# Seven-product 2x2 blocks for three more products of a fused attention and SwiGLU kernel, and silu in one ScalarE operation

## The chip, the cores and the metric

One NeuronCore of a Trainium2 chip. The metric is the device time of one execution in microseconds; less is better. Engines are named as in the profile: PE is TensorE, PEld its weight loads, DVE VectorE, ACT ScalarE, POOL GpSimd, SP the queue that issues most DMAs.

## The reference

```python
# q, k, v: 4 batches, 8 heads, 768 positions, 64 wide; heads 0, 2, 6 see all earlier keys,
# the others see the first 4 keys and the last 64
scores = scale * np.matmul(q, k.transpose(0, 1, 3, 2))
scores = np.where(mask[None, :, :, :], scores, -1000000000.0)
a = softmax(scores)
attn_out = np.matmul(a, v)
x = attn_out.transpose(0, 2, 1, 3).reshape(B * S, H * D)     # 3072 tokens x 512
g = x @ w_gate                                               # 512 x 1536
silu = g * (1.0 / (1.0 + np.exp(-g)))
val = x @ w_val                                              # 512 x 1536
out = (silu * val) @ w_out                                   # 1536 x 512
```

## The kernel before, in words

Attention runs in 24 tiles of 128 queries. For a tile, PE multiplies keys with queries into PSUM (`scores`, line 567), ACT takes the exponential (579), DVE or POOL multiply a mask in (587), PE multiplies with the values (597), DVE divides by the sum (604, 605), and the result is turned by PE (621) or by a DMA (615) into `xt`, the columns of x for the second part. Four tiles make a group of 512 tokens; there are six groups.

For a group, `gate` (759) computes 12 blocks of 128 rows of g and 12 of val, each with four matmuls of 128x128 weights and 512 columns into one bank of PSUM. The silu is computed as g (1 + tanh(g/2)) / 2: ACT takes the tanh (765), DVE multiplies (1 + tanh) by g (769, `stt1`), and a second DVE operation (775, `stt2`) multiplies by 0.5 and val into `h_sb`. The output product of a group is already done in 2x2 blocks with seven products instead of eight (`seventh`, line 860, matmuls of 256 columns): `hsum` (831) makes four sums of blocks of h on DVE or POOL, `wsum` (412) made the sums of blocks of w_out once, and `gathered` (886, 890, 898) adds the seven results into the four blocks of the output, which are stored by DMA.

Every piece of work is a `Task` with the engines it may run on, the tasks it waits for and the buffers it takes from rings. The order in which tasks are issued, the engine of each and the buffer it gets are three tables of digits at the head of the file (`ORDER`, `WAYS`, `SLOTS`), written by a planner beforehand. Each engine works through its own instructions in that order, and semaphores hold it where an input or a buffer isn't ready. The eight banks of PSUM are shared by the rings gv, o and big: a `gate` block holds its bank until the DVE operation that reads it last is done. Tasks of one group are mixed with attention of later ones and output products of earlier ones; the attention ends at about 161 us.

Of the kernel before, what the change touches and what calls it, by code (L numbers as in the profile page):

```python
# [7 lines left out]
FP = mybir.dt.float32  # L8
# [8 lines left out]
    "06000307090A0401081U0D1V1cy11W1X0C1d1f1e0B2021021g280g1i2229231h2B2A1j0m1r2C0h1Y1p1s2D1a0F1Z2N1q"  # L17
    "2X1b1k2E0G2O1l2W1t1m2F1u2L1x1v1w2f2M1n2g2c1y1oxk2h0n27242d25262e2l2i2m2G1z0E0y2H2I2P0z2Q2j8e2R2t"
    "8o0k8f112o2x8p8g302p108q2U312J0i132V8h2K8r2y050H8t8s8y8i8u2k983C8w8v8m323D8j2n2z3I0q8k9D8x991493"
    "3J8l9A3L8z8n94380l91903K96950o2Z9E929B3M979G2Y9F0I3N9C3U339H1C3R3V2a2q2r0j342b9h2s3S162u3O3W9c9i"  # L20
    "0r3T3X9j359d363b9I3P0J3E372v9J3Q3f3i1D2w9N9e0K1F3A9O9f3B3g2S3H9k0p179P3G0v9m9g393F9l9Q9n3h0s3Y3j"
    "9K3Z0u199r3u3a3c3n9R0x3l9s401G3k3m0w9L3o0L3d9M9S3v419o9u2T9t0M9T3p429U433w3q9v441A9p3r450R4C493e"
    "1B469q4A9X4H3y3s4B9Y9a479Z9V3t4D9b3x4Q4N4K9W4OAu9z480O4LAQ9y1H18AnA00tB2Av124RAz1EAw0P4EB0A1BE4Z"
    "B1Ap4V4Y4gB34FBH4GBF0NAxAq1Q1K4hBGAV5CArAkAWBIB41IAl0QAX1J15AY4eAy1S4IB7AZAm0SALAR3z4JAoB51MAs4d"
    "AS9wAt4f1RAM5DANB91TB69x5KBCB8BA4b5fBBAa0WBD5I4o4i4l4P4pA2A45l4m1LA34M5FAT0U1N5E4S5L1PAUAf4jA5A8"
    "1OAg4v5JAbAh4a4k4TAcAE5g4UA95n4y514q4c4zAAA60V4r0a6KACAB5o5GA7AF4WAdAD524n4sAGAiAeAK540TAj505T55"
    "4t5mAO4u5U5MAP565W4x5753AHBM4wBLBJBN5NAI5c5VAJ58595XBO4XBR5A5H5O5BBK5v5p5sBP5wBX5q5Y0YBQ600Z5r5Z"
    "5t5a0XBV5b6I5u6366BWCb6E6HBS645iCe5h6N67BY5PBTCC6O5QBbCD5R7O5d6PCM6wCc6v5xCd0cBZ68CECN71BcCF6JBa"
# [26 lines left out]
SLOTS = (
    "001423105578362145403027124360570705626241030877537806901020040702261213013460614010320001264002"
    "430101642120400017524426503000204102434011162426123000254004600122630164212045422322214400101000"
    "130234502420041024003014523602204224610042412422404222212503602112240050221240143404020044225200"
    "005411611104105112030140001212061231013100700167007612020117123450061751067110011241201016300460"
    "216005211560201025311267261606003611020071110012121267117601100231114700730027201774112050100016"  # L60
    "610661265014600771040126102070067023342264511137001010641241015202110066116102500050001512722100"
    "4111232013411120253127611561005111201141005015610026745406"
# [57 lines left out]
def kernel(  # L120
# [253 lines left out]
    T_w = {}  # L374
# [392 lines left out]
    def stt1(g, j, c):  # L767
        sl[g, j, c] = buf("sil", [128, 512], FP, "sil")[:, 0:c[1] - c[0]]
        nc.vector.scalar_tensor_tensor(  # L769
            out=sl[g, j, c], in0=sg.pop((g, j, c)), scalar=1.0, op0=ALU.add,  # L770
            in1=gs.pop((g, j, c)), op1=ALU.mult)

    def stt2(g, j, c):
        hs[g, j] = h_sb[:, g % 2, j]
        nc.vector.scalar_tensor_tensor(  # L775
            out=hs[g, j][:, c[0]:c[1]], in0=sl.pop((g, j, c)), scalar=0.5, op0=ALU.mult,
            in1=vs.pop((g, j, c)), op1=ALU.mult)
# [251 lines left out]

    for g in range(NG):  # L1030
        w = SIZES[g] * 128
        xs = [T_xe[t] for t in range(FIRST[g], FIRST[g + 1])]
        T_h = {}
        for j in range(NJ):
            parts = [(0, 256), (256, 512)] if g == 0 and j < HALVES else [(0, w)]
            for c in parts:
                a = P.add(f"gate{g}.{j}.{c[0]}", ["PE"],
                          (lambda g=g, j=j, c=c: gate(g, j, c, wg_sb, gs)),
                          deps=xs[c[0] // 128:c[1] // 128] + [T_w["g", j // 2][j % 2]],
                          takes=["gv"])  # L1040
                th = P.add(f"tanh{g}.{j}.{c[0]}", ["ACT"],
                           (lambda g=g, j=j, c=c: tanh(g, j, c)), deps=[a], takes=["sig"])
                s1 = P.add(f"stt1 {g}.{j}.{c[0]}", ["DVE"],
# [9 lines left out]
                T_h.setdefault(j, []).append(s2)  # L1053
                P.uses(a, "gv", s1)
                P.uses(v_, "gv", s2)
                P.uses(th, "sig", s1)
                P.uses(s1, "sil", s2)
                P.uses(T_first_x[g], "xt", a, v_)
        if g < SEVENS:
# [68 lines left out]
```

## Time and profile before

| what | before |
|---|---|
| median of 3 runs | 239.07 us (239.04 to 239.14) |
| profiled execution | 239.03 us |
| its span, first to last instruction | 237.2 us |
| PE / PEld busy | 230.5 / 146.0 us |
| DVE / ACT / POOL busy | 194.5 / 141.2 / 110.6 us |
| granted PE clock | 1.00 |
| DMA | 40.73 MB, mean 172 GB/s |

The profile is of one execution. An engine is busy while at least one of its instructions is in it; matmuls overlap, so their mean duration is longer than their spacing. "Idle before" is the engine's idle time just ahead of an instruction, with what ended it. The time outside the span (1.83 us here) belongs to the execution but to no instruction.

### The profile page before, as it was taken

To read this page: it belongs to the slowest core of one execution; us is meant where nothing else is said; L and a number is where in the kernel's file an instruction comes from. 1 tells how busy PE (TensorE), PEld (TensorE's weight loads), DVE (VectorE), ACT (ScalarE), POOL (GpSimd) and SP (SyncE) were. 2 spreads that over 40 slices of the span, in tenths; PEclk is the share of its full clock that TensorE was granted. 3 is DMA by queue.
4 is the path that set the end of the run, shared out by engine and by line. 5 is a ranking of instruction groups with operands and counts; after the bars stand their busy time and mean duration, and the time that the engine had idled before them with its cause. 6 is when DMAs were issued, how large, how long until landed. Compare 5 with 4: busy or idle time off the path is not lost.

```text
span 237.2 us, 5639 instructions
## 1 busy us (share of the span) xinstructions
PE 230.5 (97%) x2211; PEld 146.0 (62%) x2211; DVE 194.5 (82%) x362; ACT 141.2 (59%) x217; POOL 110.6 (47%) x132
## 2 busy tenths in 40 slices
PE   7899999999999999999999999999999999999994
PEld 2577865655457778655464557766555565557883
DVE  2689999998999699698968989786969867788873
ACT  3699999889599879839575485384242232231010
POOL 7386577937484940998600550884000000525500
PEclk9999999999999999999999999999999999999999
DMA  6999999999999999999798124011620000220044
GB/s 173 351 343 366 326 346 356 358 350 296 271 238 165 236 291 182 289 164 188 196 171 207 34 48 87 4 22 20 203 44 0 3 0 0 87 92 1 20 183 155
DMA packets 67194, 40.73 MB, mean 172 GB/s; under 512 B 25184, under 2 KB 61024, under 8 KB 67168
## 3 DMA queue, kind: packets, MB, share of 16 engines
q1 hardware_dynamic: 65248, 37.50, 63.4%
q10 hardware_dynamic: 1920, 2.88, 3.3%
q8 instruction: 17, 0.28, 0.5%
q14 instruction: 9, 0.07, 0.1%
HBM read 28.31 MB, written 6.29 MB: 146 GB/s over the span
## 4 chain that ended last, share of the span: by engine, by line
PE 92%; DVE 3%; DMA 2%; ACT 1%; issue 0%; DVEq 0%
PE banks L759 51%; PE banks L860 23%; PE banks L567 8%; PE banks L597 6%; PE banks L473 2%; DMA raw<-in_q_dram 2%; PE banks L621 1%; DVE wt_sb L412 1%; DVE sil L769 1%; ACT hq L206 0%; PE banks L321 0%; DVE kT L208 0%; DVE hq L212 0%; DVE qT L208 0%; DVE xb L605 0%; DVE h_sb L775 0%
## 5 line engine op out<-in xcount | busy, mean ns | idle before, releaser
L765 ACT ACTIVATE sig<-banks 128x512 f32<-128x512 f32 (+1 forms) x76 | 42.7, 574 | 54.6 <-PE banks L759 47.5
L759 PE MATMUL banks<-xt,wg_sb 128*128 128x512 f16 (+1 forms) x304 | 71.4, 368 | 0.5 <-DVE sil L769 0.5
L759 PE MATMUL banks<-xt,wv_sb 128*128 128x512 f16 (+1 forms) x304 | 70.9, 368 | 0.0
L579 ACT ACTIVATE e<-banks 128x1024 f16<-128x1024 f32 (+2 forms) x68 | 59.5, 910 | 15.0 <-PE banks L567 6.3
L769 DVE SCALAR_TENSOR_TENSOR sil<-sig,banks 128x512 f32<-128x512 f32 (+1 forms) x76 | 48.8, 655 | 14.3 <-ACT sig L765 13.6
L775 DVE SCALAR_TENSOR_TENSOR h_sb<-sil,banks 128x512 f16<-128x512 f32 (+1 forms) x76 | 48.9, 655 | 2.8 <-PE banks L759 1.8
L860 PEld LDWEIGHTS <-h_sb 128*128 128x128 f16 x420 | 40.4, 98 | 8.5
L759 PEld LDWEIGHTS <-wv_sb 128*128 128x128 f16 x304 | 28.6, 98 | 26.9
L759 PEld LDWEIGHTS <-wg_sb 128*128 128x128 f16 x304 | 28.1, 98 | 27.2 <-issue 0.8
L587 POOL TENSOR_TENSOR e<-e,m 128x640 f16<-128x640 f16 (+1 forms) x17 | 28.0, 1655 | 19.8 <-ACT e L579 19.4
L831 POOL TENSOR_TENSOR h_sb<-h_sb 128x768 f16<-128x768 f16 x13 | 21.2, 1640 | 22.5 <-DVE hs_sb L831 16.7
L898 DVE TENSOR_TENSOR out_sb<-banks,out_sb 128x512 f32<-128x512 f32 x37 | 25.1, 688 | 7.4 <-PE banks L860 7.0
L860 PE MATMUL banks<-wt_sb,h_sb 128*128 128x256 f16 x216 | 26.2, 273 | 0.0
L831 POOL TENSOR_TENSOR hs_sb<-h_sb 128x768 f16<-128x768 f16 x3 | 4.9, 1639 | 45.1 <-PE banks L860 41.2
L860 PE MATMUL banks<-wo_sb,h_sb 128*128 128x256 f16 x204 | 25.1, 273 | 0.0
L597 PEld LDWEIGHTS <-e 128*128 128x128 f16 x472 | 18.0, 97 | 5.8 <-DVE e L587 0.2
L567 PEld LDWEIGHTS <-kT 64*128 64x128 f16 x472 | 14.4, 94 | 9.3 <-issue 8.7
L567 PE MATMUL banks<-qT,kT 64*128 64x128 f16 x472 | 19.7, 218 | 0.2 <-ACT qT L206 0.2
L597 PE MATMUL banks<-vt,e 128*128 128x65 f16 x472 | 19.7, 193 | 0.1
L206 ACT CAST hq<-raw 128x1024 f16<-128x1024 f32 (+1 forms) x16 | 14.7, 936 | 5.2 <-DMA raw<-in_q_dram 3.2
L605 DVE TENSOR_TENSOR xb<-banks,rc 128x512 f16<-128x512 f32 x24 | 16.6, 692 | 0.8
L208 POOL CAST vt<-raw 64x512 f16<-64x512 f32 x23 | 14.0, 607 | 2.3 <-DMA raw<-in_v_dram 1.3
(64 smaller groups left out, 192.9 us busy)
## 6 DMA issues: line engine op xcount, KB each, us to landing
raw<-in_v_dram SPq DMA_DIRECT2D x12, 512.0 KB, 5.8
raw<-in_q_dram SPq DMA_DIRECT2D x8, 512.0 KB, 6.2
raw<-in_k_dram SPq DMA_DIRECT2D x8, 512.0 KB, 5.3
raw<-in_moe_w_gate_dram SPq DMA_DIRECT2D x6, 512.0 KB, 8.6
raw<-in_moe_w_val_dram SPq DMA_DIRECT2D x6, 512.0 KB, 8.2
raw<-in_moe_w_out_dram SPq DMA_DIRECT2D x6, 512.0 KB, 7.9
out_dram<-out_sb SPq DMA_DIRECT2D x6, 512.0 KB, 4.4
raw<-in_q_dram SPq DMA_DIRECT2D x8, 256.0 KB, 6.4
```

The costliest lines, as they stand in the source:

```text
L567: nc.tensor.matmul(sc[:, c:c + n, :], weights, moving, start=first, stop=last)
L579: nc.scalar.activation(out=to, in_=src, func=AF.Exp, scale=scale)
L587: ENG[task().way].tensor_tensor(out=ev, in0=ev, in1=mm, op=ALU.mult)
L597: nc.tensor.matmul(avs[t][:, odd, n * 66:n * 66 + 65], ee, vv, start=(m == 0), stop=(m == len(bl) - 1))
L605: nc.vector.tensor_tensor(out=xb.rearrange("p n o d -> p o n d"), in0=av[:, :, :, 0:64], in1=rc.to_broadcast([128, 2, 4, 64]), op=ALU.mult)
L759: nc.tensor.matmul(ps, wsb[:, kk, j * 128:(j + 1) * 128], xt[:, kk, c[0]:c[1]], start=(kk == 0), stop=(kk == 3))
L765: nc.scalar.activation(out=sg[g, j, c], in_=gs[g, j, c], func=AF.Tanh, scale=0.5)
L769: nc.vector.scalar_tensor_tensor(out=sl[g, j, c], in0=sg.pop((g, j, c)), scalar=1.0, op0=ALU.add, in1=gs.pop((g, j, c)), op1=ALU.mult)
L775: nc.vector.scalar_tensor_tensor(out=hs[g, j][:, c[0]:c[1]], in0=sl.pop((g, j, c)), scalar=0.5, op0=ALU.mult, in1=vs.pop((g, j, c)), op1=A ...
L831: ENG[T_hs[g, x][part].way].tensor_tensor(out=to, in0=a, in1=b, op=op)
L860: nc.tensor.matmul(rooms[g, p][:, x, lo:hi], left[:, j, 128 * x:128 * x + 128], right[:, j, lo:hi], start=(on is None and (j == 0 if apart ...
L898: nc.vector.tensor_tensor(out=cell(*to), in0=room, in1=plus, op=ALU.add)
```

## The change

For groups 4 and 5 the values, and for group 5 the gates too, are computed in 2x2 blocks: x of a group is split in two halves of 256 tokens and two halves of the 512 inputs, the weights in two halves of the inputs and two of the 1536 outputs. The work goes in three slices of 2 x 128 rows from each half of the outputs. For a slice, seven products (`w_product`, line 1118 of the changed kernel) of 4 matmuls with 256 columns take the place of the 4 blocks of 4 matmuls with 512 columns. Four sums of blocks of x per group (`xsum`, 1098) and, once for each matrix, four sums of blocks of the weights in two pieces each (`msum`, 1068) are made by DVE or POOL. Products 1, 6, 7 and 4 accumulate in one bank, X, and what stands there between them is copied out (`w_copy`, 211 on DVE and 209 on ACT) before the next may add; products 5 and 3 share another bank, Z, with an add (`w_add`, 1139) between them; product 2 has the third, Y. The sums lie in float32 tiles of the ring raw. The cells are r1 and u2, u3 (copies of X), y2 (copy of Y), c11 = r1 + y2, c21 (copy of X at the end), c22 = u3 + Z, c12 = u2 + Z.

For groups 4 and 5 the silu is one ACT operation, `Silu` (784 from the gate's bank, in place; 1164 from the cells), and the DVE operation (1 + tanh) g is gone; `stt2` takes 1.0 in place of 0.5. These wait until the last exponential of the attention is done. All three tables are new, so the order of everything else is new as well, and some tasks change their engine.

```diff
-    "06000307090A0401081U0D1V1cy11W1X0C1d1f1e0B2021021g280g1i2229231h2B2A1j0m1r2C0h1Y1p1s2D1a0F1Z2N1q"
+    "07000306090A0401080Dy11W1U1V0C1X1c1f0B201d211e1g280g1i2229231h022B2A1j0m1r2C0h1Z1p1s2D1a0F1Y2N1q"
...
+    def silu(g, j, c):
+        if g in WINO["v"]:
+            to = gs[g, j, c]
+        else:
+            to = buf("sil", [128, 512], FP, "sil")
+        nc.scalar.activation(out=to, in_=gs.pop((g, j, c)), func=AF.Silu)
+        sl[g, j, c] = to
+
     def stt2(g, j, c):
         hs[g, j] = h_sb[:, g % 2, j]
         nc.vector.scalar_tensor_tensor(
-            out=hs[g, j][:, c[0]:c[1]], in0=sl.pop((g, j, c)), scalar=0.5, op0=ALU.mult,
+            out=hs[g, j][:, c[0]:c[1]], in0=sl.pop((g, j, c)),
+            scalar=1.0 if g in SILU else 0.5, op0=ALU.mult,
             in1=vs.pop((g, j, c)), op1=ALU.mult)
...
+    WINO = {"v": (4, 5), "g": (5,)}
+    SILU = (4, 5)
...
+    def msum(mat, i, kk):
...
+        if i in (1, 3):
+            a, b = MB[mat, i // 2, 1][:, kk], MB[mat, 0, i // 2][:, kk]
+        else:
+            a, b = MB[mat, 1, 1 if i == 2 else 0][:, kk], m_sums[mat, i // 2, kk]
+        ENG[T_mw[mat, i][kk].way].tensor_tensor(
+            out=m_sums[mat, i, kk], in0=a, in1=b, op=ALU.subtract)
...
+    def xsum(g, i):
...
+        a, b, op = {1: (A[1, 0], A[1, 1], ALU.add), 2: (Z[:, 0], A[0, 0], ALU.subtract),
+                    3: (A[0, 0], A[1, 0], ALU.subtract),
+                    4: (A[0, 1], Z[:, 1], ALU.subtract)}[i]
+        ENG[T_xs[g, i].way].tensor_tensor(out=Z[:, i - 1], in0=a, in1=b, op=op)
+
+    W_ON = {1: "X", 6: "X", 7: "X", 4: "X", 2: "Y", 5: "Z", 3: "Z"}
+
+    def w_product(mat, g, s, p):
...
+        on = mat, g, s, W_ON[p]
+        begins = p in (1, 2, 5)
+        if begins:
+            w_rooms[on] = buf("gv", [128, 2, 256], FP, "gv")
+        for m in range(2):
+            at = slice(128 * (2 * s + m), 128 * (2 * s + m) + 128)
+            for kk in range(2):
+                if p <= 3:
+                    right = MB[mat, p > 1, p > 2][:, kk, at]
+                else:
+                    right = m_sums[mat, {4: 4, 5: 1, 6: 2, 7: 3}[p], kk][:, at]
+                nc.tensor.matmul(
+                    w_rooms[on][:, m], right, left[:, kk],
+                    start=(begins and m == 0 and kk == 0), stop=(kk == 1),
+                    skip_group_check=True)
...
+    def w_copy(mat, g, s, name):
+        to = w_cell(mat, g, s, name)
+        copy(T_wc[mat, g, s, name], to, w_rooms[mat, g, s, "Y" if name == "y2" else "X"])
+
+    def w_add(mat, g, s, name):
+        to = w_cell(mat, g, s, name)
+        other = w_cell(mat, g, s, "y2") if name == "c11" else w_rooms[mat, g, s, "Z"]
+        ENG[T_wc[mat, g, s, name].way].tensor_tensor(out=to, in0=other, in1=to, op=ALU.add)
...
+    def silu_w(g, j):
+        c = (0, 512)
+        ring = "gv" if g in WINO["v"] else "sil"
+        sl[g, j, c] = buf(ring, [128, 512], FP, ring)
+        nc.scalar.activation(out=by_halves(sl[g, j, c]), in_=w_cells("g", g, j), func=AF.Silu)
...
+            p1 = product(1, xs + w_lo)
+            r1 = copied("r1", [p1])
+            p6 = product(6, [r1, T_xs[g, 2]] + T_mw[mat, 2])
+            u2 = copied("u2", [p6])
+            p7 = product(7, [u2, T_xs[g, 3]] + T_mw[mat, 3])
+            u3 = copied("u3", [p7])
+            p4 = product(4, [u3] + T_mw[mat, 4])
+            p2 = product(2, xs + w_lo)
+            y2 = copied("y2", [p2, r1])
+            P.uses(p2, "gv", y2)
+            c11 = added("c11", [y2])
+            c21 = copied("c21", [p4, c11])
+            P.uses(p1, "gv", c21)
+            p5 = product(5, [T_xs[g, 1]] + T_mw[mat, 1])
+            c22 = added("c22", [p5, u3])
+            p3 = product(3, [c22, T_xs[g, 4]] + w_hi)
+            c12 = added("c12", [p3])
+            P.uses(p5, "gv", c12)
```

Two places of the new order. The first is on ACT, where group 4's gates begin and the attention has ended. Before, there are only the tanh operations into `sig` and one store:

```order
L765 ACTIVATE sig_2858<-banks_87 128x512
L579 ACTIVATE e_2861<-banks_87 128x1024
L919 DMA out_0_dram<-out_sb_94 128x2x512
L765 ACTIVATE sig_2882<-banks_87 128x512
L765 ACTIVATE sig_2941<-banks_87 128x512
```

Now, from the last exponential (`e`) on, with the copies of cells (`raw`), an `ACT_TABLE_LOAD`, and the silu operations from a bank into the same bank:

```order
L582 ACTIVATE e_2875<-banks_87 128x1024
L209 COPY raw_2882<-banks_87 128x512
L209 COPY raw_2899<-banks_87 128x512
L209 COPY raw_2882<-banks_87 128x512
L209 COPY out_sb_94<-banks_87 128x2x256
L209 COPY raw_2952<-banks_87 128x512 x2
L209 COPY raw_2899<-banks_87 128x512
L934 DMA out_0_dram<-out_sb_94 128x2x512
L784 ACT_TABLE_LOAD
L784 ACTIVATE banks_87<-banks_87 128x512 x3
L209 COPY raw_2801<-banks_87 128x512
L784 ACTIVATE banks_87<-banks_87 128x512
```

The tanh operations of groups 4 and 5 are gone from ACT, and seven copies of cells stand between the last exponential and the fourth silu, with the load of a second function table ahead of the first.

The second place is the end of POOL, with the sums of h for the last output products (`hs_sb` is the first sum, which product 5 reads; `h_sb` and `raw` the others). Before:

```order
L831 TENSOR_TENSOR h_sb_92<-h_sb_92 128x3x256
L831 TENSOR_TENSOR hs_sb_93<-h_sb_92 128x768 x2
L831 TENSOR_TENSOR h_sb_92<-h_sb_92 128x3x256 x3
L831 TENSOR_TENSOR hs_sb_93<-h_sb_92 128x768
L831 TENSOR_TENSOR h_sb_92<-h_sb_92 128x3x256
```

Now, from the last two c11 adds (`raw`) on; the first `h_sb` row is group 4's, the two together are group 4's and group 5's:

```order
L1139 TENSOR_TENSOR raw_3357<-raw_3357 128x512
L1139 TENSOR_TENSOR raw_3389<-raw_3389 128x512
L846 TENSOR_TENSOR h_sb_92<-h_sb_92 128x3x256
L846 TENSOR_TENSOR hs_sb_93<-h_sb_92 128x768
L846 TENSOR_TENSOR h_sb_92<-h_sb_92 128x3x256 x2
L846 TENSOR_TENSOR hs_sb_93<-h_sb_92 128x768
L846 TENSOR_TENSOR raw_3613<-h_sb_92 128x768 x2
```

Both halves of group 5's first sum are on POOL now, where the last one alone was, and the sums into `raw` came over from DVE. PE's order of group 5's output products goes from 1, 7, 6, 2, 5, 4, 2, 3, 3 to 1, 5, 7, 6, 2, 4, 2, 3, 3 (products 2 and 3 in halves).

More of the change, by code (lines that the diff above doesn't have):

```diff
@@ new lines @@
+    T_mw = {}
+    for mat in ("v", "g"):
+        for i in range(1, 5) if WINO[mat] else []:
+            T_mw[mat, i] = []
+            for kk in range(2):
+                before = T_mw[mat, i // 2][kk:kk + 1] if i in (2, 4) else []
+                T_mw[mat, i].append(P.add(
+                    f"vw{i}.{kk}" + mat, ["DVE", "POOL"],
+                    (lambda mat=mat, i=i, kk=kk: msum(mat, i, kk)),
+                    deps=[y for n in range(6) for y in T_w[mat, n]] + before,
+                    takes=(["hq"] if i == 4 else ["e"]) if mat != EARLY
+                    else [] if kk else ["raw"],
+                    after=T_mw[mat, i][:1]))
@@ new lines, in stt2_w, with sums_of_x @@
+    def stt2_w(g, j):
+        hs[g, j] = h_sb[:, g % 2, j]
+        nc.vector.scalar_tensor_tensor(
+            out=by_halves(hs[g, j]), in0=by_halves(sl.pop((g, j, (0, 512)))),
+            scalar=1.0 if g in SILU else 0.5, op0=ALU.mult, in1=w_cells("v", g, j), op1=ALU.mult)
+    T_xs, T_wp, T_wc = {}, {}, {}
+    def sums_of_x(g, xs):
+        first = T_first_x[g]
+        for i in range(1, 5):
+            T_xs[g, i] = P.add(
+                f"xs{g}.{i}", ["DVE", "POOL"], (lambda i=i: xsum(g, i)),
+                deps=xs + {2: [T_xs.get((g, 1))], 4: [T_xs.get((g, 2))]}.get(i, []),
+                takes=[] if i > 1 else ["raw"], after=[T_xs[g, 1]] if i > 1 else [])
+            P.uses(first, "xt", T_xs[g, i])
+        sum1 = T_xs[g, 1]
+        P.uses(sum1, "raw", T_xs[g, 2], T_xs[g, 4])
@@ L1036 @@
             for c in parts:
[L1037 to L1043, printed above, removed]
-                           (lambda g=g, j=j, c=c: stt1(g, j, c)), deps=[th], takes=["sil"])
+                below = ("c11", "c21") if j < NK else ("c12", "c22")
@@ new lines @@
+                was = [T_p[g - 2, p] for p in ((6, 7) if j < NK else (3, 4))] if g > 1 else []
+                was += T_hs[g - 2, 4] if g > 1 and j < NK else []
+                if g not in SILU and g not in WINO["g"]:
+                    P.uses(th, "sig", s1)
+                if g in WINO["v"]:
+                    cells = [T_wc["v", g, j % NK // 2, y] for y in below]
+                    s2 = P.add(f"stt2 {g}.{j}.{c[0]}", ["DVE"],
+                               (lambda g=g, j=j: stt2_w(g, j)), deps=[s1] + cells + was)
+                    T_h.setdefault(j, []).append(s2)
+                    P.uses(holder if g in SILU else th if g in WINO["g"] else a, "gv", s2)
+                    P.uses(T_wc["v", g, j % NK // 2, head], "raw", s2)
+                    continue
@@ L1048 @@
                            takes=["gv"])
-                was = [T_p[g - 2, p] for p in ((6, 7) if j < NK else (3, 4))] if g > 1 else []
-                was += T_hs[g - 2, 4] if g > 1 and j < NK else []
                 s2 = P.add(f"stt2 {g}.{j}.{c[0]}", ["DVE"],
```

219 lines of the change are left out of this document (174 added, 45 removed).

## The prediction

> **What bounds the kernel now.** I read the page first: busy times, slices, and the chain that ended last.
>
> ```profile
> span 237.2 us, 5639 instructions
> ...
> PE 230.5 (97%) x2211; PEld 146.0 (62%) x2211; DVE 194.5 (82%) x362; ACT 141.2 (59%) x217; POOL 110.6 (47%) x132
> ...
> PEclk9999999999999999999999999999999999999999
> ...
> PE 92%; DVE 3%; DMA 2%; ACT 1%; issue 0%; DVEq 0%
> ```
>
> PE is busy for 97% of the span at full clock, and 92% of the last chain is PE. Busy does not yet mean saturated, because matmuls overlap. So the second view is the busy time by stretches, and the third the timeline of PE in the last stage, where the row length and count give the spacing.
>
> ```profile
> core 0: us, PE busy (x) PEld busy (x) DVE busy (x) ACT busy (x) POOL busy (x), PEclk, DMA share, GB/s
> ...
> 161.00:233.70 72.70, 72.70 (x513) 46.41 (x511) 57.20 (x98) 17.89 (x30) 13.34 (x9) 1.00 0.18 58
> ```
> ```profile
> 180.59 1.47 PE L860 MATMUL banks<-wo_sb,h_sb 128*128 128x256 f16 x12
> 181.90 1.89 PE L759 MATMUL banks<-xt,wg_sb 128*128 128x512 f16 x8
> ```
> ```profile
> L759 PE MATMUL banks<-xt,wv_sb 128*128 128x512 f16 x100 | 24.5, 379 | 0.0
> L759 PE MATMUL banks<-xt,wg_sb 128*128 128x512 f16 x96 | 23.5, 379 | 0.0
> L860 PEld LDWEIGHTS <-h_sb 128*128 128x128 f16 x216 | 21.1, 98 | 4.6
> ...
> L860 PE MATMUL banks<-wo_sb,h_sb 128*128 128x256 f16 x108 | 13.4, 273 | 0.0
> L860 PE MATMUL banks<-wt_sb,h_sb 128*128 128x256 f16 x108 | 13.1, 273 | 0.0
> ...
> L860 PE MATMUL banks<-wt_sb,hs_sb 128*128 128x256 f16 x36 | 4.4, 273 | 0.0
> ...
> L860 PE MATMUL banks<-wo_sb,raw 128*128 128x256 f16 x12 | 1.5, 272 | 0.0
> ```
>
> One matmul of 512 columns lasts 379 ns, and eight in a row take 1.89 us: (1890 - 379) / 7 = 216 ns from start to start. Twelve of 256 columns take 1.47: (1470 - 273) / 11 = 109 ns. From 161 us on (this third view is the groups of that stretch alone) there are 196 of the first and 264 of the second: 42.3 + 28.8 = 71.1 us of the 72.7, and the 53 small matmuls of the last attention tiles fill the rest. PE has no slack here; what is taken from it comes off the end, unless something else is late.
>
> **What the change takes from PE.** Three products of a group with a matrix (values of groups 4 and 5, gates of group 5) had 12 blocks of 4 matmuls with 512 columns; now 3 slices of 7 products, each of 4 matmuls with 256 columns. Out: 3 x 48 = 144 x 0.216 = 31.10 us. In: 3 x 84 = 252 x 0.109 = 27.47. That is **-3.64 us**, if every new matmul keeps the pace. The new ones load a 128x128 weight block each; that row lasts 98 ns, less than the 109 between matmuls, and the 264 above already run so.
> The Trainium skill (TensorE: Matmul & The Clock Gate, section Back-to-back issue gap) gives about 81 ns per matmul at 128 columns and 131 at 512 as the sustained pace of a real kernel; this trace disagrees, 216 at 512.
>
> **What it adds on the other engines.** Prices:
>
> ```profile
> 206.59 0.69 DVE L898 TENSOR_TENSOR out_sb<-banks,out_sb 128x512 f32<-128x512 f32 x1
> 207.19 0.68 DVE L769 SCALAR_TENSOR_TENSOR sil<-sig,banks 128x512 f32<-128x512 f32 x1
> 207.78 0.68 DVE L775 SCALAR_TENSOR_TENSOR h_sb<-sil,banks 128x512 f16<-128x512 f32 x1
> ```
> ```profile
> L831 DVE TENSOR_TENSOR h_sb<-hs_sb,h_sb 128x768 f16<-128x768 f16 x11 | 6.0, 551 | 0.0
> ...
> L412 POOL TENSOR_TENSOR wt_sb<-wo_sb 128x512 f16<-128x512 f16 x3 | 3.5, 1159 | 0.1
> ...
> L206 ACT COPY raw<-banks 128x512 f32<-128x512 f32 x1 | 0.6, 585 | 9.4 <-PE banks L860 9.4
> ```
>
> DVE starts such operations 0.60 apart when they queue. By the order, DVE loses 24 first products of the silu (24 x 0.60 = 14.4 us) and 6 sums of h that go to POOL (-2.8, taking 0.47 each, the 0.551 less a similar overlap), and gains 12 copies, 18 adds from a bank and 3 of SBUF (33 x 0.60 = 19.8), 6 sums of weights (2.8) and 3 of x (1.2): **+6.6 us**. Against 57.2 busy of 72.7 that makes 63.8 of 69.1, if all of it falls there. ACT gains 33 copies (19.3 us) on 17.9, and has room. POOL gains 6 h sums, 10 weight sums, 5 x sums and 6 adds in f32; no row has an f32 add on POOL. I bound it by 1.16 (the f16 of the same shape) and twice that, and take 1.2. None of the three reaches 69, so all is hidden as a total; what can show is latency, in three places.
>
> **First, the chained banks.** Products 1, 6, 7 and 4 add into one bank, and a copy of each intermediate must be read out before the next may add; product 3 waits likewise for an add on product 5. The price of such a hop:
>
> ```profile
> 228.31 0.82 PE L860 MATMUL banks<-wo_sb,h_sb 128*128 128x256 f16 x6
> ...
> 229.17 0.37 ACT L206 COPY out_sb<-banks 128x256 f32<-128x256 f32 x1 [2.69 <-PE banks L860]
> ```
> ```profile
> 61.00 1.27 DVE L769 SCALAR_TENSOR_TENSOR sil<-sig,banks 128x512 f32<-128x512 f32 x2
> 61.73 1.02 PE L759 MATMUL banks<-xt,wg_sb 128*128 128x512 f16 x4 [0.50 <-DVE sil L769]
> ```
>
> The bank's last matmul ends 0.164 after the next could start (273 - 109), ACT starts 0.04 later (229.13 to 229.17), copies for 0.585, and PE goes 0.05 after the release (61.68 to 61.73): 0.84 us on ACT, 0.94 on DVE, if the engine is free. There are 36 hops. Counting PE's rows between them in the new order, 22 have 2.2 us or more of other PE work, six 1.74, six 1.31, one 1.06, and one 0.86 (one gate of group 4 between products 7 and 4 of slice 0). So each fits when the copying engine is free; an operation in its way (0.5 to 0.6) delays the eight tightest by 0.1 to 0.5 each. Bounds 0 and 8 x 0.25 = 2.0; I take **0.3**, near the lower end, as ACT, the engine with room, has four of the eight and both of the tightest; DVE has the other four.
>
> **Second, the table load.** The order of ACT has a second load ahead of the first silu, and it waits there for that gate's bank. Nothing of the first load can be seen but its length:
>
> ```profile
> L206 ACT ACT_TABLE_LOAD x1 | 1.3, 1283 | 0.7 <-PEq L1109 0.7
> ```
> ```profile
> L765 ACT ACTIVATE sig<-banks 128x512 f32<-128x512 f32 x24 | 14.0, 597 | 37.9 <-PE banks L759 33.8 <-DVE sil L769 4.1
> ```
>
> No row has Silu; I price it as the Tanh of that shape, 0.597 (bounds: the copy's 0.585, and 0.811 of a 768-wide Exp). From the end of gate 0 of group 4: 0.2 to the load, 1.28, two silus (0.6 and 0.5), product with the values for the second about 0.8, release 0.05: 3.4 us until that bank is free. PE reaches the product that takes it after two gates and three block products, 2 x 0.864 + 3 x 0.436 = 3.04. So **0.4 us** shows, 0 if DVE is quicker, 1.3 if all the load does.
> The Trainium skill (ScalarE: Activation LUTs, section What ACT_TABLE_LOAD costs) states 1283 ns and a drain of 1380; the row agrees with the first, and no run here shows the second. By it, 1.4 us more would show.
>
> **Third, the end.** After the fifth product of group 4's output, POOL has four sums in a row (the sum of h for group 5, two rows of h_sb, the second half of that sum), and product 5 of group 5 waits for the last.
>
> ```profile
> 214.74 3.23 POOL L831 TENSOR_TENSOR h_sb<-h_sb 128x768 f16<-128x768 f16 x2 [5.67 <-DVE h_sb L831]
> ```
>
> Four are 6.46 us, and with 0.2 and 0.05 at the ends 6.7. PE has five products of 12 x 0.109 = 1.31 in that time, 6.55. So **0.2** shows; 0 to 1.6, the upper end if one more sum is ahead.
>
> **The front** swaps the first two loads and puts the first mask fills on ACT.
>
> ```profile
> 9.12 0.62 PE L473 MATMUL banks<-ident,hq 128*128 128x128 f16 x8 [0.81 <-DVE hq L212]
> ```
>
> PE waits here for the cast of the second query load, the third in either order, and this cast stays on DVE: **0**, with -0.8 and +0.8 (the wait gone or doubled) as bounds. The 0.50 at 61.7 us above may go with the new order, or come back elsewhere: 0, or -0.5.
>
> **The sum** is made against the profiled execution, 239.03 us (span 237.2 and 1.8 around it), 0.04 under the median of the runs. -3.64 + 0.3 + 0.4 + 0.2 = -2.74: **236.3 us**. The lower end is -3.64 - 0.5, 234.9. For the upper, hops near their bound, 0.4 and 0.4 for the others: -3.64 + 2.0 + 0.8 = -0.84, 238.2.
>
> **The rivals.**
> 1. DVE's queue is late at the hops, partly: the total of 92% speaks for it, the room on ACT against. Stalls of 1.8 to 3.1 in place of 0.9: 237.2 to 238.5. Chance 0.11.
> 2. The table load shows twice its length, since what follows a load is covered in the trace by a wait: +1.28, 237.6. Chance 0.05. By the drain that the Trainium skill states (ScalarE: Activation LUTs, same section) it is 1.38, 237.7.
> 3. Slower: DVE is two operations behind throughout the last two groups, so a hop takes 0.9 + 1.2 = 2.1 us. Then the tight ones miss by 1.24, 1.04, six by 0.8 and six by 0.36: 9.2 us; as one stall lets the queue catch up for the next, about half, 4.6: 239.03 - 3.64 + 4.6 = 240.0. It decides from 0.10 us a hop (3.64 / 36). For it: the DVE total. Against: DVE at 79% in the same stretch never delayed PE there. Chance 0.08.
> 4. The new matmuls don't keep 109 ns, weight loads show: 252 x 0.098 = 24.7 more, 260. The 264 rows at 109 ns speak against it. Chance 0.02. By the paces of the Trainium skill (TensorE: Matmul & The Clock Gate, same section), an estimate: 144 x 0.131 = 18.9 out, 252 x 0.098 (a third of the way from 81 to 131) = 24.7 in, +5.8, 244.8.
> 5. The change does on PE what it says, but the new order loses it elsewhere (front +0.8, hops 2.0, the load 0.8): within 0.2% of before. Chance 0.06.
>
> **Chances.** The forecast keeps 0.68. A difference of 0.2%, 0.48 us, is about what a measurement of this kernel can tell from none. Faster: 0.68 + 0.11 + 0.05 = 0.84; within: 0.06; slower: 0.08 + 0.02 = 0.10. The range leaves out cases 3 to 5 and the top of case 1, 0.2 in all.
>
> **What would show it.** Right: the block matmuls at 109 ns (four take 0.60), 252 of them, PE idle in the last 70 us under 1 us, most of it after the table load, and DVE about 90% busy there. Wrong: idle of PE before block products put down to copies or adds on DVE (rivals 1 and 3), a wait of 2 us after the table load (2), block matmuls further apart (4), or a later start at 9 us (5).

## The result

| kernel | median us (runs) | ratio to before, 95% interval | span of the profiled run, us |
|---|---|---|---|
| before | 239.10 (238.97 to 240.37, 6) | | 237.2 |
| changed | 237.15 (237.06 to 238.45, 6) | 0.9917 [0.9888, 0.9945] | 235.4 |
| changed, run again with the experiments | 237.42 (236.96 to 238.21, 6) | 0.9937 [0.9925, 0.9949] | 235.5 |

The change makes the kernel 0.6 to 0.8% faster, 1.6 to 2.0 us. The forecast was 236.3, range 234.9 to 238.2: sign and range hold, and the gain is a third smaller than forecast. The two medians of the changed kernel lie 0.3 us apart, so differences of a few tenths are read from the profiles below, not from the medians. The profiled execution took 237.17 us.

First the totals in the page of the changed kernel:

```profile
PE 227.4 (97%) x2319; PEld 156.7 (67%) x2319; DVE 198.6 (84%) x363; ACT 164.6 (70%) x265; POOL 149.6 (64%) x156
...
PE 80%; DVE 7%; DMA 2%; issue 1%; ACT 1%; ACTq 0%; DVEq 0%
```

PE still sets the end, at the same granted clock (1.00). But its share of the chain that ended last has gone from 92% to 80%, and DVE's from 3% to 7%: the chain now leaves PE for a while where it went straight through before. Where it does is in the last stretch. Its window up to the end of the last matmul (PE, PEld, DVE, ACT and POOL busy, clock, DMA share, GB/s), and that of the last group without the end of its output:

```profile
core 0: us, PE busy (x) PEld busy (x) DVE busy (x) ACT busy (x) POOL busy (x), PEclk, DMA share, GB/s
161.00:231.76 70.76, 69.91 (x628) 57.01 (x625) 61.47 (x104) 36.89 (x66) 46.64 (x31) 1.00 0.19 58
200.00:225.60 25.60, 25.60 (x236) 22.84 (x234) 24.77 (x41) 15.13 (x28) 18.37 (x12) 1.00 0.19 69
```

The stretch takes 70.76 us in place of 72.70: 1.94 less, which is all of the gain (239.03 to 237.17 is 1.86). The exchange of matmuls was worth 3.64, so 1.70 came back within the stretch. PE, which had no idle time there before, has 0.85 now, and POOL works 46.64 us in place of 13.34. The second row says what the first hides: DVE, 87% busy on average over the stretch, is 97% busy from 200 to 225.6 us, where PE is busy all the time. Two engines are full there at once. PE's idle time stands in three places, as the waits of the whole program show (us in total, times, longest; left out are three rows on L324 and L476, which belong to the first 10 us):

```profile
PE banks L875 <- DVE raw L901: 0.4, 1, 0.4
PE banks L1118 <- DVE h_sb L1168: 0.3, 1, 0.3
PE banks L600 <- DVE e L590: 0.2, 1, 0.2
```

Note what isn't there: no wait of PE for a copy or an add of the chained cells (L209, L211 or L1139 into raw). The three waits of the last stretch, each in its timeline (start, duration, instruction, in brackets the idle time ahead of it and what ended it), are these.

**At 161.9**, a mask of the attention's last tile:

```profile
159.87 1.65 POOL L1068 TENSOR_TENSOR raw<-wv_sb 128x768 f16<-128x768 f16 x1
160.22 0.68 DVE L789 SCALAR_TENSOR_TENSOR h_sb<-sil,banks 128x512 f16<-128x512 f32 x1
...
160.81 1.05 DVE L590 TENSOR_TENSOR e<-e,m 128x640 f16<-128x640 f16 x1
...
161.57 0.20 PE L600 MATMUL banks<-vt,e 128*128 128x65 f16 x1
...
161.92 0.66 PE L600 MATMUL banks<-vt,e 128*128 128x65 f16 x16 [0.15 <-DVE e L590]
```

From the one start of PE to the next are 0.35 us where the pace is 0.03: 0.32 lost. (The bracket gives less, since the matmul before is counted busy until it has drained. So every loss below is taken from start to start.) DVE's mask took 1.05 us, beside one of the change's sums of weights on POOL (L1068). DVE's other operation beside the same sum, L789 with one input in a bank, took its usual 0.68.

**At 177.8**, behind the second table load:

```profile
174.47 1.28 ACT L784 ACT_TABLE_LOAD   x1 [0.75 <-PE banks L762]
...
175.76 1.56 ACT L784 ACTIVATE banks<-banks 128x512 f32<-128x512 f32 x3
...
176.43 1.29 DVE L1168 SCALAR_TENSOR_TENSOR h_sb<-banks,raw 128x512 f16<-128x512 f32 x2 [0.51 <-issue]
...
176.83 0.60 PE L1118 MATMUL banks<-raw 128*128 128x256 f16 x4
...
177.77 0.49 PE L1118 MATMUL banks<-raw 128*128 128x256 f16 x3 [0.34 <-DVE h_sb L1168]
```

Load, silu, product with the values, release of the bank, matmul: the path of the prediction's second term, row by row. The last matmul of the row at 176.83 starts at 177.16; to the next are 0.61 where the pace is 0.109: 0.50 lost.

**At 230.3**, in the last output:

```profile
222.85 0.38 ACTq L934 DMA_DIRECT2D out_dram<-out_sb  x1
...
223.44 0.39 SPq L934 DMA_DIRECT2D out_dram<-out_sb  x1
...
227.58 0.69 DVE L913 TENSOR_TENSOR out_sb<-banks,raw 128x512 f32<-128x512 f32 x1 [1.94 <-DMA out_dram<-out_sb]
...
228.82 0.69 DVE L913 TENSOR_TENSOR out_sb<-banks,out_sb 128x512 f32<-128x512 f32 x1 [0.55 <-DMA out_dram<-out_sb]
...
229.55 0.69 DVE L901 TENSOR_TENSOR raw<-banks,out_sb 128x512 f32<-128x512 f32 x1
...
230.29 1.47 PE L875 MATMUL banks<-wo_sb,raw 128*128 128x256 f16 x12 [0.36 <-DVE raw L901]
```

The sums of group 5's output may not write out_sb until the stores of group 4's have read it. DVE waits for these twice, the sum L901 queues behind, and PE waits for the bank that L901 reads: 0.52 lost.

### The profile page after: what moved, and what is told of

Same layout as the page of the kernel before. It is cut to its first block, busy times and chain, and to the rows that moved or that the text cites. A ratio compares the mean times of both kernels' runs of the same rounds, so it can differ in the third digit from the quotient of the medians.

```text
span 235.4 us, 5938 instructions
## 1 busy us (share of the span) xinstructions
PE 227.4 (97%) x2319; PEld 156.7 (67%) x2319; DVE 198.6 (84%) x363; ACT 164.6 (70%) x265; POOL 149.6 (64%) x156
## 4 chain that ended last, share of the span: by engine, by line
PE 80%; DVE 7%; DMA 2%; issue 1%; ACT 1%; ACTq 0%; DVEq 0%
PE banks L762 38%; PE banks L875 19%; PE banks L1118 11%; PE banks L570 6%; PE banks L600 5%; DMA out_dram<-out_sb 2%; DVE out_sb L913 2%; DVE h_sb L789 1%; DVE xb L608 1%; PE banks L476 1%; DVE e L590 1%; PE banks L624 1%; DVE h_sb L1168 1%; ACT L784 1%; DVE h_sb L846 0%
## 5 line engine op out<-in xcount | busy, mean ns | idle before, releaser
L762 PE MATMUL banks<-xt,wg_sb 128*128 128x512 f16 (+1 forms) x256 | 58.9, 366 | 0.0
L762 PE MATMUL banks<-xt,wv_sb 128*128 128x512 f16 (+1 forms) x208 | 47.4, 363 | 0.0
L762 PEld LDWEIGHTS <-wg_sb 128*128 128x128 f16 x256 | 24.0, 98 | 21.7 <-POOL wg_sb L211 0.2
L775 DVE SCALAR_TENSOR_TENSOR sil<-sig,banks 128x512 f32<-128x512 f32 (+1 forms) x52 | 32.8, 641 | 6.5 <-ACT sig L768 5.6
L768 ACT ACTIVATE sig<-banks 128x512 f32<-128x512 f32 (+1 forms) x52 | 28.5, 564 | 11.3 <-PE banks L762 8.9
L789 DVE SCALAR_TENSOR_TENSOR h_sb<-sil,banks 128x512 f16<-128x512 f32 (+1 forms) x52 | 32.8, 640 | 2.1 <-PE banks L762 1.3
L590 POOL TENSOR_TENSOR e<-e,m 128x1024 f16<-128x1024 f16 (+1 forms) x15 | 26.7, 1785 | 10.2 <-ACT e L582 9.8
L762 PEld LDWEIGHTS <-wv_sb 128*128 128x128 f16 x208 | 19.0, 98 | 17.4
L209 ACT COPY raw<-banks 128x512 f32<-128x512 f32 x34 | 19.1, 590 | 14.7 <-PE banks L1118 13.4
L1168 DVE SCALAR_TENSOR_TENSOR h_sb<-banks,raw 128x512 f16<-128x512 f32 x24 | 16.0, 683 | 2.4 <-ACT banks L784 1.5
L211 POOL CAST vt<-raw 64x512 f16<-64x512 f32 x24 | 14.5, 608 | 2.5 <-DMA raw<-in_v_dram 1.5
```

What stands on the lines that cost most here:

```text
L590: ENG[task().way].tensor_tensor(out=ev, in0=ev, in1=mm, op=ALU.mult)
L762: nc.tensor.matmul(ps, wsb[:, kk, j * 128:(j + 1) * 128], xt[:, kk, c[0]:c[1]], start=(kk == 0), stop=(kk == 3))
L768: nc.scalar.activation(out=sg[g, j, c], in_=gs[g, j, c], func=AF.Tanh, scale=0.5)
L775: nc.vector.scalar_tensor_tensor(out=sl[g, j, c], in0=sg.pop((g, j, c)), scalar=1.0, op0=ALU.add, in1=gs.pop((g, j, c)), op1=ALU.mult)
L789: nc.vector.scalar_tensor_tensor(out=hs[g, j][:, c[0]:c[1]], in0=sl.pop((g, j, c)), scalar=1.0 if g in SILU else 0.5, op0=ALU.mult, in1=vs ...
```

## The experiments

The reasons to be tested: PE sets the end at an unchanged pace, and what is missing of the 3.64 us went into these three waits. Against it stand two others: DVE's queue at the chained banks, and the pace of the block matmuls.

**The changed kernel again**, as the yardstick. 

> The changed kernel once more, on the chip on which its three variants run, so that differences of half a microsecond can be read against it. Every theory expects 237.15 us, within 0.3.

237.42 us, ratio 0.9937. By the starts of PE's matmuls the same three waits cost 0.32, 0.50 and 0.39 us here, the last one 0.13 less than in the first execution.

**The table loaded early.**

```
+        if (mat, g, s, name) == ("v", 4, 0, "u3"):
+            nc.scalar.activation(out=early, in_=early, func=AF.Silu)
...
+    early = const.tile([128, 1], FP, name="early")
...
```

> A silu of one element per partition is put on ScalarE right behind its copy of the third intermediate of group 4's first slice, so that the second table is loaded in ScalarE's idle time there; results are the same. The theory: the load stands between gate 0 of group 4 and the release of its bank, and TensorE's wait of 0.50 us at 177.2 us is its price. Without it the wait goes and the end comes 0.5 us earlier: 236.65. The rival, that the chained banks and the queues of VectorE set the end of this stretch: the wait only moves, 237.1 as before. If the load hits a copy that a chained product waits for, up to 0.8 later.

236.68 us, ratio 0.9901 [0.9888, 0.9913], span 234.9 in place of 235.4 or 235.5. The wait at 177.8 is gone. The small silu on ACT, with the load right ahead of it, and DVE's first products with the values:

```profile
172.83 0.20 ACT L1136 ACTIVATE early<-early 128x1 f32<-128x1 f32 x1
...
175.81 1.28 DVE L1170 SCALAR_TENSOR_TENSOR h_sb<-banks,raw 128x512 f16<-128x512 f32 x2
```

DVE's product starts 0.62 earlier than in the changed kernel. The wait in the last output is 0.60 here, where the changed kernel has 0.52 and 0.39: everything comes earlier there, except the landing of the stores. Two executions of one kernel differ by more than this step, so that reading is likely but not shown.

**Cells of their own for the last output.**

```
-    def cell(x, y):
-        return out_sb[:, x, :, HM * y:HM * y + HM]
+    out5 = wg_sb.rearrange("p a n -> p (a n)")[:, 0:4 * DM * 2].bitcast(FP).rearrange(
+        "p (x s n) -> p x s n", x=2, s=2)
+
+    def cell(x, y, g=0):
+        return (out5 if g == NG - 1 else out_sb)[:, x, :, HM * y:HM * y + HM]
...
```

> The last group's four output cells get memory of their own (that of the gate weights, which are no longer read by then), so that VectorE's sum no longer waits for group 4's stores. The theory: TensorE's wait of 0.52 us at 229.7 us is the wait of VectorE for the landing of these stores, 1.94 us at 227.6, passed on through its queue. It should go: 236.65. The rival, the prediction's own, is that GpSimd's four sums for this output are late there: no gain, 237.1.

236.26 us, ratio 0.9885 [0.9871, 0.9899], span 234.5. The waits of DVE for the stores and of PE at 230.3 are gone, while POOL's sums, the rival, are where they were. In the timeline POOL's first sum, then DVE's sum that waited 0.55 for a store, and the one behind it:

```profile
221.27 1.65 POOL L846 TENSOR_TENSOR hs_sb<-h_sb 128x768 f16<-128x768 f16 x1
...
227.97 0.69 DVE L916 TENSOR_TENSOR wg_sb<-banks,wg_sb 128x512 f32<-128x512 f32 x1
...
228.69 0.69 DVE L904 TENSOR_TENSOR raw<-banks,wg_sb 128x512 f32<-128x512 f32 x1
```

L904 (L901 of the changed kernel) starts 0.86 earlier. The span is 0.9 shorter, more than the wait: of the 0.9, 0.63 lie ahead of the end of the last matmul (231.13 in place of 231.76), 0.1 of that already in the first 10 us, where executions differ; 0.24 lie behind the last matmul, with the last stores, and their cause stays open.

**One weight sum on DVE.**

```
-        ENG[T_mw[mat, i][kk].way].tensor_tensor(
+        way = "DVE" if (mat, i, kk) == ("v", 3, 1) else T_mw[mat, i][kk].way
+        ENG[way].tensor_tensor(
...
```

> One of the sixteen weight sums, the second half of the third for the values, goes from GpSimd to VectorE, at the same place in the program's order; results are the same. The theory: VectorE's mask at 160.81 us took 1.05 us in place of 0.48 because GpSimd's sum ran at the same time, and TensorE waits 0.32 us for it. With the sum on VectorE the mask takes 0.48 again, and the wait goes if the sum's own 0.55 lies behind the mask: 236.85, at best. If the sum lies ahead of the mask, the mask ends as late as now, in another way: 237.1. The rival, that the mask is slow for a reason of its own: it still takes 1.05.

236.61 us, ratio 0.9899 [0.9886, 0.9911], span 234.9. With no sum on POOL beside it, the mask takes its 0.48 us, and PE passes without a wait:

```profile
160.71 0.48 DVE L590 TENSOR_TENSOR e<-e,m 128x640 f16<-128x640 f16 x1
...
161.46 0.69 PE L600 MATMUL banks<-vt,e 128*128 128x65 f16 x17
```

**All three edits together.** 

> The three edits together: the second table loaded early, cells of their own for the last group's output, and the weight sum on VectorE. The theory, that the waits at 161.6, 177.2 and 229.7 us are independent and TensorE sets the end between them: their 0.32, 0.50 and 0.52 us (0.60 by the runs with one edit, where the stores' landing had become the later end) go together, -1.4 from 237.3: 235.9. The rival, that one wait takes the place of another: 236.3, as with the cells alone.

235.77 us, ratio 0.9857 [0.9839, 0.9875], span 234.1: better than each alone and than both kernels. The runs of before that stand beside it had a median of 239.49, so the ratio says more than the time: 1.43% under before, twice the changed kernel's gain. In the last output nothing waits for a store (out_sb's place is taken by wg_sb here):

```profile
226.80 0.69 DVE L916 TENSOR_TENSOR wg_sb<-banks,raw 128x512 f32<-128x512 f32 x1 [1.71 <-PE banks L875]
```
```profile
161.00:230.69 69.69, 69.57 (x631) 56.92 (x627) 62.16 (x105) 37.38 (x67) 45.95 (x30) 1.00 0.20 60
```

PE is idle for 0.12 us of 69.69 in the whole last stretch. This rest stands at the second place, at 177.22. DVE's products with the values and PE's next weight load:

```profile
175.90 1.27 DVE L1174 SCALAR_TENSOR_TENSOR h_sb<-banks,raw 128x512 f16<-128x512 f32 x2
...
177.22 0.31 PEld L1122 LDWEIGHTS <-raw 128*128 128x128 f16 x3 [0.29 <-issue]
```

From start to start of PE's matmuls 0.28 of the 0.50 are still lost there: the mask no longer holds PE up, so PE comes 0.3 earlier, and DVE's product, which releases the bank, ends at 177.17, no earlier than in the run with the early load alone (175.81 + 1.28, 177.09). So the three waits have three causes, and each goes with its own edit; but they are not independent, and for 0.28 us the rival was right. The time met the expectation all the same, partly by luck: 0.24 us went behind the last matmul too, as with the cells alone, and the expectation had not counted that.

**Eight products in place of seven.**

```
-        for m in range(2):
+        for m in [0, 1, 0, 1] if p == 2 else range(2):
```

> The second product of each slice is issued twice (eight products in place of seven): 36 more block matmuls, and the output is the same. The theory, TensorE sets the end through the whole last stage at 0.109 us for each of them: +3.92 us, 241.1. The rival, that the chained banks or VectorE set the pace and TensorE has slack: clearly less, 237.5 to 239. The other rival, that weight loads show in the block matmuls at a pace that the neighbours hide: more than 4.5.

240.99 us, ratio 1.0088 [1.0069, 1.0107]: 3.6 to 3.8 over the changed kernel, for 3.92 of matmuls. PE sets the end, and at 109 ns. The rivals, clearly less or more than 4.5, fall. By the starts of PE's rows the wait at 230.3 is gone here (0.52) and 0.28 more is lost around 178: 3.92 - 0.52 + 0.28 = 3.68.

**Six products.**

```
+        for m in [] if p == 3 else range(2):
```

> The matmuls of the third product are left out (six products in place of seven; the upper right block of the result lacks that product): 36 fewer block matmuls. The theory, TensorE sets the end: -3.92 us, 233.2, less what the adds and copies, which all stay, then no longer hide. The rival, that VectorE at 61.5 busy of 70.8 us is near to setting the end itself: it would be at 61.5 of 66.9, and less than half of the 3.9 is gained, 235.2 or more.

235.86 us, ratio 0.9896 [0.9836, 0.9956]: only 1.3 to 1.6 of the 3.92 are gained. Its last stretch, the parts from 180 and from 200 us on, and two of PE's waits:

```profile
161.00:230.66 69.66, 67.11 (x589) 53.31 (x589) 61.10 (x104) 36.74 (x66) 46.56 (x31) 1.00 0.19 60
180.00:200.00 20.00, 19.14 (x153) 14.59 (x151) 17.14 (x28) 8.66 (x17) 14.09 (x10) 1.00 0.01 2
200.00:222.00 22.00, 21.24 (x190) 18.24 (x188) 21.30 (x36) 14.87 (x28) 18.23 (x12) 1.00 0.13 49
```
```profile
177.68 0.60 PE L1118 MATMUL banks<-raw 128*128 128x256 f16 x4 [0.78 <-DVE h_sb L1168]
...
182.85 0.38 PE L1118 MATMUL banks<-xt,wv_sb 128*128 128x256 f16 x2 [0.67 <-DVE h_sb L1168]
```

PE's idle time goes from 0.85 to 2.55 us, for two reasons. From 200 us on DVE is busy for 21.30 of 22.00 us (97%) and sets the pace. The last of DVE's sums of h, on which POOL's final two wait, ends at 225.06 where it ended at 225.64, although PE has 3.92 less to do ahead of it. But by the starts of PE's matmuls, 2.0 of the 3.0 us that this run loses beyond the changed kernel lie ahead of 200 us, where DVE is busy for 85 and 86% (16.20 of 19.00 us from 161 to 180, 17.14 of 20.00 from there on). There PE waits for banks that DVE's products with the values release late: 0.94 at 177.68, behind the table load, where the changed kernel loses 0.50, and 0.83 at 182.85, where it loses nothing. That is a path that PE's work had hidden, and not a full DVE. The expectation of the theory (up to 3.9) was far off. The rival had the number, but its reason, DVE's total, holds only from 200 us on.

**The silu alone**, in the kernel before: one operation of ACT for all blocks of the last two groups but one.

```
+        if one(g, j):
+            nc.scalar.activation(out=sl[g, j, c], in_=gs.pop((g, j, c)), func=AF.Silu)
+            return
...
```

> The kernel before, with the silu of the last two groups in one operation of ScalarE (but for one block, which stands ahead of the last softmax), nothing else changed: VectorE has 23 x 0.60 = 13.8 us less to do there. The theory, TensorE sets the end and VectorE at 79% delayed nothing: 239.1, 0 to 0.5 later for a table load. The rival, that part of the gain came from the relief of VectorE: 0.5 to 2 us faster.

239.45 us, ratio 1.0016 [1.0004, 1.0027]. DVE is relieved by a quarter of its work, and nothing is gained:

```profile
161.00:234.12 73.12, 72.87 (x513) 46.49 (x511) 43.84 (x75) 19.17 (x31) 13.35 (x9) 1.00 0.18 58
```
```profile
169.11 1.28 ACT L775 ACT_TABLE_LOAD   x1 [2.36 <-DVE h_sb L783]
...
170.40 0.60 ACT L775 ACTIVATE sil<-banks 128x512 f32<-128x512 f32 x1
...
171.05 1.02 PE L759 MATMUL banks<-xt,wv_sb 128*128 128x512 f16 x4 [0.24 <-ACT sil L775]
```

DVE is 43.84 busy in place of 57.20. The 0.4 us of difference is again PE behind the table load. So the relief alone is worth nothing in the kernel before. That it pays for what the blocks add to DVE is an inference, from the runs below that give DVE more work.

**The blocks with the silu in two operations again**, tanh and a product, at the place where the one operation stood.

```
...
+        nc.scalar.activation(out=th, in_=g_, func=AF.Tanh, scale=0.5)
+        nc.vector.scalar_tensor_tensor(out=to, in0=th, scalar=1.0, op0=ALU.add, in1=g_, op1=ALU.mult)
...
```

> The blocks as they are, but the silu of the last two groups is made in two operations again, a tanh on ScalarE and a product on VectorE; results are the same within rounding. VectorE gets back 24 x 0.60 = 14.4 us: 61.5 + 14.4 = 75.9 in a stretch of 70.8. The theory that VectorE now has little room left: it becomes the bound, and the time is 5 to 10 us longer, 242 to 247. The rival, that VectorE's load matters little since ScalarE can share: 239 at most.

263.2 us, ratio 1.1019 [1.0959, 1.1079], far beyond both. The stretch, and the first of its waits:

```profile
161.00:258.20 97.20, 77.61 (x639) 59.32 (x637) 84.61 (x130) 37.23 (x67) 48.81 (x31) 0.95 0.15 42
```
```profile
177.28 0.70 DVE L1053 SCALAR_TENSOR_TENSOR banks<-sig,banks 128x512 f32<-128x512 f32 x1 [0.60 <-ACT sig L1052]
...
180.89 0.68 DVE L1149 TENSOR_TENSOR raw<-banks,raw 128x512 f32<-128x512 f32 x1
...
181.62 1.01 PE L1128 MATMUL banks<-raw,wv_sb 128*128 128x256 f16 x4 [4.13 <-DVE raw L1149]
```

DVE isn't full either (84.61 of 97.20), and PE's granted clock is 0.95 in this stretch, where PE stands still for 20 us. DVE stands in its queue waiting for one tanh after the other, and the add of a chained bank, on which PE waits 4.13 us, stands behind these. So the run doesn't show DVE's total as the bound; it shows an order that was written for another program. What a replanned version would take stays open.

**DVE's work alone**, with no new wait: the products with the values issued twice, for all twelve blocks of the last group and then for four.

```
+        for again in range(2 if g == 5 else 1):
...
+        for again in range(2 if g == 5 and j % 3 == 1 else 1):
...
```

> VectorE issues each product of silu and value of the last group twice, the second with the same result: 12 operations of 0.6 us, 7.2 us, with no new wait on another engine. This tells load from latency in the run with the silu in two operations, where VectorE had 24 more operations, each of them behind a tanh of ScalarE. The theory, that VectorE's total decides: 61.5 + 7.2 = 68.7 of 70.8, still under TensorE; 237.3 to 238.3. The rival, that the queue's order decides and each operation in the way of a chained bank is paid at once: 3 us or more, 240 to 244.

244.03 us, ratio 1.0210 [1.0177, 1.0242], 6.6 to 6.9 over the changed kernel.

```profile
200.00:232.50 32.50, 27.11 (x233) 22.24 (x231) 31.93 (x52) 15.42 (x28) 18.40 (x12) 1.00 0.13 46
```

DVE is 98% busy, and PE 83%: DVE sets the pace. My sum for this run was wrong, since it set 7.2 us against the room of the whole stretch, where all of it falls behind 200 us. The rival got the number, but the total explains it as well (7.8 more busy from 161 us on, 0.8 free), so the next run was to tell them apart.

> As the run before with products issued twice, but only four of the twelve (blocks 1, 4, 7 and 10 of the last group): 4 x 0.66 = 2.6 us more for VectorE. From 200 us on VectorE is busy 28.2 of 31.8 us in the changed kernel; 12 more of them (7.9 us) could not fit there and cost 6.9. Four do fit, with 30.8 of 31.8. The theory, that the total of this stretch decides: 0 to 0.6 later than the changed kernel, 237.3 to 237.9. The rival, that each operation delays a chained bank or a product that TensorE waits for, with or without room in the total: 4/12 of 6.9 = 2.3 later, 239.6.

239.33 us, ratio 1.0010 [0.9997, 1.0022], 1.9 to 2.2 over the changed kernel.

```profile
200.00:227.70 27.70, 25.84 (x233) 22.50 (x231) 26.87 (x45) 15.70 (x29) 18.38 (x12) 1.00 0.14 51
```

The rival's number again (2.3 was expected). But the window that I took for the total was still too wide: it reached to 231.76, and DVE waits for matmuls and stores in its last 6 us. Up to 225.6 DVE has 24.77 of 25.60, room for 0.83, and from 161 us on its busy time went from 61.47 to 64.49 in this run: 3.0 - 0.8 = 2.2. So the total of DVE, over the window in which it is full, gives the same as the rival's queue, and the two aren't told apart by this run. PE's new losses stand at four places, from start to start 0.53 at 205.32, 0.75 at 210.92, 0.62 at 220.30 and 0.61 at 222.22; only the second is put down to the add of a chained bank. What both say is the same for the use: in the last group DVE has under 1 us left.

## Why the prediction was right, and where it was off

**The exchange on PE, -3.64: held.** Eight products cost 3.6 to 3.8 for 3.92, and the block matmuls run at the pace of the rows that it was priced by (0.60 for four). Rival 4 falls. Its price by the Trainium skill's paces of 131 and 81 ns (TensorE: Matmul & The Clock Gate, section Back-to-back issue gap) gave 244.8; the trace has 216 ns at 512 columns and 109 at 256 instead.

**The chained banks, 0.3: too high; they cost nothing that the trace shows.** No wait of PE in the changed kernel is put down to a cell's copy or add, and by the starts of PE's matmuls no block product but the one at 177.8 begins more than 0.05 late. What is left of the 1.70 us beside the three waits is 1.70 - 0.32 - 0.50 - 0.52 = 0.36. Of this, 0.10 are lost at 162.52, right behind the mask, and go with its wait when the weight sum is on DVE; 0.08 are lost at 213.18, ahead of an output product; the rest, 0.18, lies in smaller steps and in what falls on either side of the border at 161 us, and is not traced. The time lies at the low end of rival 1's range (237.2 to 238.5), but its mechanism, stalls at the hops, is not what gave it. Rival 3 did not happen.

**The table load, 0.4: right, 0.50.** The path was the one written down, and the early load takes it away. From the end of gate 0 to the freed bank are 3.37 us (174.40 to 177.77; 3.4 was forecast). On PE's side the 3.04 run from the start of the row at 174.23, which is 0.17 ahead of that end, and so 2.87 count: this is the 0.1 by which the term was short. Rival 2 falls: nothing shows twice. The load takes 1.28 us, and the next ACTIVATE starts 0.01 after its end (174.47 + 1.28, then 175.76; in the silu alone 169.11 + 1.28, then 170.40). So the drain of 1380 ns that the Trainium skill states (ScalarE: Activation LUTs, section What ACT_TABLE_LOAD costs) is not seen behind the load in these two runs. Nor is it seen ahead of one: in the run with the early load, the load starts 0.01 after the end of the copy before it (170.93 + 0.59, then 171.53).

**The end, 0.2: the step that failed.** "After the fifth product of group 4's output, POOL has four sums in a row ..., and product 5 of group 5 waits for the last." It doesn't wait: the second half of the sum is ready and PE goes on. The weight loads that read the old sum, POOL's first and last of the four new ones, and product 5:

```profile
215.25 1.30 PEld L875 LDWEIGHTS <-hs_sb 128*128 128x128 f16 x12
...
216.59 1.64 POOL L846 TENSOR_TENSOR hs_sb<-h_sb 128x768 f16<-128x768 f16 x1 [0.50 <-PE banks L875]
...
221.39 1.64 POOL L846 TENSOR_TENSOR hs_sb<-h_sb 128x768 f16<-128x768 f16 x1
...
223.22 1.47 PE L875 MATMUL banks<-wt_sb,hs_sb 128*128 128x256 f16 x12
```

POOL is done at 223.03, 0.19 ahead. The sizes were right (6.44 us for the four sums, 6.55 for PE's five products); the start was wrong. The prediction let POOL begin 0.2 after PE goes over from the fifth product of group 4 to the next (216.67), that is at 216.87. It began at 216.59, 0.04 after the last weight load that reads the old sum (216.55), while the matmuls of that product ran to 216.83. What costs 0.52 there is another mechanism, the stores of group 4, which still read out_sb when group 5 wants to write it; the prediction followed no store. Cells of their own removed the wait with POOL's sums untouched.

**A term that was missing, 0.32.** The prediction added up POOL's new sums and adds and found room on POOL. It took them as independent of DVE. They are not (see the last section), and one fell beside a mask that PE waits for.

**The totals: right in the result, too coarse as a reason.** DVE came out at 61.47 of 70.76 (forecast 63.8 of 69.1), and in the changed kernel it is hidden: "None of the three reaches 69, so all is hidden as a total". But 70 us is no stage. From 200 to 225.6 us DVE is at 97%, and the runs show what that means: four operations more on DVE cost 1.9 to 2.2, and 3.92 off PE gain only 1.3 to 1.6, a third of the missing part being lost there. The forecast came through with 0.8 us to spare, a margin that it had not worked out.

**The rest.** The front was priced at 0, and PE's matmuls behind the cast of the second query load start 0.14 earlier (8.98 in place of 9.12). The stall of 0.50 at 61.7 us went, as one of its two cases had it; yet outside the last stretch the changed kernel is 0.08 longer, so that as much was lost again elsewhere ahead of 161 us, and where is not traced. Of the signs that were to show it, PE's idle time under 1 us came (0.85), but not most of it is the table load's (0.34); DVE was to be about 90% busy and was 87%. Of the 0.88 between forecast and profiled time, 0.32 is the missing term, 0.52 - 0.2 = 0.32 the end and 0.10 the load; the 0.3 for the hops did not come. That leaves 0.44: 0.10 and 0.08 for the two small losses above, 0.08 outside the stretch, and 0.18 that is not traced.

## What to carry to other kernels

When a change takes work off the engine that sets the end, follow, at each place where that engine takes a buffer or reads a result, everything that must have happened before, stores that still read a buffer included; and take another engine's total over the stage in which both are busy, not over the whole stretch (87% here, 97% in the part that counted). When work moves to an idle engine, ask what it shares with the engines that aren't idle. And once it is done, list the bounding engine's waits in the changed stretch, measured from start to start of its instructions (its idle time left out 0.16 to 0.17 us of each wait here), and take them away one by one: here three small edits doubled the gain.

## What the runs showed of the hardware

An operation of DVE with both inputs in SBUF and one of POOL exclude each other; they don't run side by side at a lower speed. In the kernel with eight products, DVE's rows and POOL's:

```profile
172.09 1.18 DVE L1098 TENSOR_TENSOR raw<-xt,raw 128x512 f16<-128x512 f16 x1
...
191.62 1.79 DVE L1068 TENSOR_TENSOR hq<-wg_sb,e 128x768 f16<-128x768 f16 x1
```
```profile
171.71 1.27 POOL L1139 TENSOR_TENSOR raw<-raw 128x512 f32<-128x512 f32 x1
...
191.36 1.64 POOL L1068 TENSOR_TENSOR hq<-wg_sb,e 128x768 f16<-128x768 f16 x1
192.96 1.96 POOL L846 TENSOR_TENSOR h_sb<-h_sb 128x768 f16<-128x768 f16 x1
```

POOL's first operation ends at 172.98, and DVE's 0.29 later, after 1.18 us; POOL's second at 193.00, and DVE's 0.41 later, after 1.79 where it takes 0.55 alone. The mask at 160.81 ends 0.34 after POOL's sum (159.87 + 1.65), where it takes 0.48 alone. In these rows DVE's operation that comes second ends 0.29, 0.34 or 0.41 us after POOL's first (for 512, 640 and 768 elements), whether it took 0.57 us longer than alone (the mask) or 1.24. It goes the other way too: POOL's last row starts while DVE's is running and takes 1.96 in place of 1.64, ending 1.51 after DVE's end at 193.41. DVE's operation L789 with one input in a bank was not held (0.68, above). The Trainium skill says so (SBUF — State Buffer, section Who interferes with whom): a DVE instruction with two SBUF inputs contends with a GpSimd instruction that reads SBUF, and the loser blocks for the whole of it; the runs agree, but for 0.14 us of the later one's own time (0.48 - 0.34, 0.55 - 0.41), which it needn't wait with.

A silu of 128x512 on ACT took 588 ns on average from a bank and 602 from the cells, like the tanh of that shape that it was priced by (597), and POOL's f32 add of 128x512 took 1.27 where it had to wait for nobody, near the 1.2 that was taken.
